# Contractions over 128 rows in four tiles and one bank, projections set ahead, and outputs scaled behind the next block's copies

## The chip, the cores and the metric

One core of one Trainium2 chip runs one program that holds the whole computation. The metric is the device time of one execution in microseconds; the kernel before takes 2904.78 us, the median of three runs. The core has five engines with queues of their own, which run in order: TensorE (matmuls, PE in the profile, with its weight loads as PEld), VectorE (DVE), ScalarE (ACT), GpSimd (POOL) and SyncE (SP). In this kernel SP only issues transfers (DMAs), and POOL issues some and does some arithmetic. Matmuls write into a memory of their own, PSUM, in banks; a bank takes 512 fp32 columns here.

## The reference

Four layers follow each other: attention, a state-space convolution (S4D), attention, and the convolution again, with the same weights in both rounds. Sequence length is 2048, width 640, 32 heads of 20 channels, and 128 states per channel.

```python
def _A_ref(x, wqkv, wo):
    qkv = (x @ wqkv).reshape(B, S, 3, H, Dh)          # q, k, v
    scores = jnp.einsum("bhqd,bhkd->bhqk", q, k) * (Dh ** -0.5)
    p = _softmax(scores, axis=-1)
    o = jnp.einsum("bhqk,bhkd->bhqd", p, v)
    return o.reshape(B, S, D) @ wo

def _B_ref(u, log_A_real, A_imag, C_real, C_imag, log_dt, D_skip):
    P = jnp.exp((A * dt[:, None])[:, :, None] * pos[None, None, :])
    K = 2.0 * jnp.einsum("dn,dnl->dl", C, P).real     # 640 kernels of length 2048
    ...                                               # y = causal convolution of u with K, by FFT
    return y + u * D_skip

x = x + _A_ref(_layernorm(x), A_wqkv, A_wo)
x = x + _B_ref(_layernorm(x), ...)
x = x + _A_ref(_layernorm(x), A_wqkv, A_wo)
x = x + _B_ref(_layernorm(x), ...)
```

## The kernel before

**Attention.** Heads go in groups of four (`g`, 8 groups), queries in blocks of 512 (`qb`, 4 for each group), keys in tiles of 128 (`kt`, 16). A *block* is one group and one query block, 32 of them in a layer. For each key tile there are two *waves* (`j`), each for two heads: `scores` issues eight fp16 matmuls (L769) into one of two score buffers `S` of two banks each, and one exponential on ScalarE (L772) takes it to `pt`. So a layer has 1024 waves, and a key tile is a pair of them. `values` (L786) then multiplies `pt` with the values of the key tile for all four heads, in eight tiles of 64 rows and 32 columns, into two accumulators `pa`; a last column of ones gives the sum that the softmax divides by. When a block ends, DVE copies `pa` into `oc` and adds its two halves (`values`, the part under `kt == NI - 1`). The sums then travel: POOL writes them to memory (`dn<-oc`), loads them in another shape (`dr<-dn`), DVE inverts them, POOL writes them back (`dn<-dr`) and spreads them over partitions (`db<-dn`), DVE scales (`oc<-oc,db`) and POOL stores the output (`ot<-oc`). Each step is a function in the list `later` with the planned time at which it is emitted.

**Work set between the waves.** Two kinds of work share two more banks `m0` and `m1`. *Projections* (`jobs`, L560 and L524): the queries and keys of the later head blocks, 15 steps of eight matmuls into both banks for each 512 columns, 120 steps for a block of 128 channels, and the values of later heads over all 128 rows in one bank. When the queries and keys of a block are done, `norms` (L488) sums their squares, and `shift` writes one number per query and head to memory (`qm<-mr` on POOL). The loads of queries for a head group (`load_q`, on SP) read it again as `qop<-qm`. *Contractions* (`contract`, L322), in the first attention layer alone: the S4D kernel `K` is a sum over 128 states, made of factors that DVE multiplies out (`kgen`, tiles `ka` and `kb`) and TensorE contracts. There are 80 contractions of two halves each. A half has four accumulation steps, for each of which four channels stand in four column tiles and the 128 states are cut into two halves of 64 rows, each with its own bank; DVE copies the first bank to `ko` and adds the second.

**What sets the order.** The program is straight-line. The class `Plan` holds planned times of TensorE, ScalarE and DVE. `slot` puts one step between the waves if it fits before the planned end of the exponential. A contraction is taken first, but only where the planned projection time spent so far (`spent`) has reached `ahead(wave)`, a line through the pairs of wave and microseconds of `AHEAD`; otherwise the next projection step goes. A head group asks (`need`) for its projections ten key tiles into the group's last block before it, and what is missing is then emitted at once. `emptied` notes when each bank is free. TensorE, DVE, POOL and SP keep the order in which the program emits; L74 in the profile is the helper that records every operation of DVE, POOL and SP, so these are told apart by their tiles.

**Behind attention** come the output projection, in the first round together with the transform of the S4D kernel, and then the convolution.

Of the kernel before, what the change touches and what calls it, by code (L numbers as in the profile page):

```python
# [11 lines left out]
F32 = mybir.dt.float32  # L12
# [9 lines left out]
P = 128  # L22
# [7 lines left out]
NA, NB = 32, 64  # L30
LV = [1.0, 2.0, 4.0, 8.0, 16.0, 32.0, 64.0, 128.0, 256.0, 512.0, 1024.0, 1536.0]
PB = 7
AHEAD = ((0, 0.0), (108, 22.0), (364, 47.0), (490, 72.0), (740, 125.0))
WS = 256.0
LG = 2
BOUND = 30.0
# [45 lines left out]
def mha_s4d_kernel(ctx, tc, x_in, wqkv, wo, lar, aim, cr, ci, ldt, dsk,  # L82
                   c_e1, c_eb, c_f2, c_fa, c_sel, c_lv, c_id, c_sg, c_e16, c_f16, c_id16, out, parts="asas", general=None):
    nc = tc.nc
    plan = Plan()
# [8 lines left out]
    se, te = nc.scalar, nc.tensor  # L94
# [11 lines left out]
    def pst(pool, *a, **k):  # L106
        return ps_[pool].tile(*a, **k)
# [68 lines left out]
    def chain(ins):  # L176
        last[0] = tie(ins, last[0])

    def kgen():
# [126 lines left out]
            ve.tensor_mul(ts[3], fa[1], fb[0])  # L306
            yield

        def contract(bs, sub, ko, a, b):

            ps = [pst("M", [P, 512], F32, tag=f"m{r}", name=f"m{r}")[:, :DC // 4 * NB].rearrange("p (c b) -> p c b", b=NB)
                  for r in range(2)]
            for c8 in range(DC // 4):
                if c8:
                    yield plan.pe + 0.7, 0.43, True, ()
                plan.on_pe(0.43)
                for n in range(4):
                    for j in range(4):
                        ch, dd = DC * (sub % 2) + 4 * c8 + j, 4 * c8 + j
                        for r in range(2):  # L320
                            rows = slice(64 * r, 64 * r + 64)
                            chain(te.matmul(ps[r][32 * j:32 * j + 32, c8, :], a[n // 2][rows, ch, :], b[n][rows, dd, :],  # L322
                                            start=(n == 0), stop=(n == 3), tile_position=(64 * r, 32 * j)))
            kos = ko[:, 2 * sub:2 * sub + 2, :]
            emptied(lambda: ve.tensor_copy(kos, ps[0]), lambda: ve.tensor_add(kos, kos, ps[1]))
            if sub == BC // DC - 1:
                ge.dma_start(kd[bs, :].rearrange("(c j) (a b) -> (j a) c b", j=4, b=NB), ko)

# [46 lines left out]
    def emptied(*copies):  # L375

        for r, f in enumerate(copies):
            if f:
                plan.dve = max(plan.dve, plan.pe + 0.25)
                f()  # L380
                free[r] = plan.dve + 0.15
# [12 lines left out]
    def attention(x, stats):  # L394
# [228 lines left out]
        def slot(until=None):  # L623
# [3 lines left out]
            begun = head[0] and head[0][2]  # L627
            if pend and part[0] is None and not begun and (head[0] is None or spent[0] >= ahead(len(ends) - 2)):
                t, f, args = pend[0]
                t = max(t + 0.15, *free)  # L630
                if t <= plan.pe or until is None and head[0] is None:
                    part[:] = f(*args), (t, 0.43, True, ())
                    pend.pop(0)
            step = part[1] if part[0] else head[0]
            if step is None:
# [14 lines left out]
        def drain_later(end=False):  # L650
            send(end)
            while later and (later[0][0] <= plan.pe or end):
                later.pop(0)[1]()
# [103 lines left out]
        plan.keep = True  # L757
        pp = c.enter_context(tc.tile_pool(name="pp", bufs=PB))
        ev = c.enter_context(tc.tile_pool(name="ev", bufs=2))
        ready = []  # L760

        def scores(kt_, kc, qt):

# [14 lines left out]
        def values(qb, g, kt, pts, pa):  # L778
# [10 lines left out]
            if kt == NI - 1:  # L789
# [6 lines left out]
                ve.tensor_copy(oc, pa[0])  # L796
                ve.tensor_add(oc, oc, pa[1])
                sums_[0] = plan.dve + 0.15

                def sums():  # L800
                    for j in range(4):
# [17 lines left out]

                def scale():  # L820
                    ve.tensor_mul(oc, oc, db[0])

                def store():
                    for j in range(4):
                        h = 4 * g + j
                        ge.dma_start(ot[h * DH:(h + 1) * DH, 512 * qb:512 * qb + 512], oc[32 * j:32 * j + DH, :])
                later.extend((plan.dve + n, f) for n, f in (
                    (0.2, sums), (5.0, load), (10.0, invert), (11.0, back), (15.5, spread), (22.5, scale), (23.8, store)))
                later.sort(key=lambda e: e[0])

        def end_jobs():

# [67 lines left out]
                    tail = end_jobs()  # L900
        for r_ in ready:
            values(*r_[1:])
        drain_later(True)
        plan.keep = False
        first.append(split(1))
# [501 lines left out]
```

## Time and profile before

| | |
|---|---|
| median of three runs | 2904.78 us (2903.93 to 2905.59) |
| the profiled execution | 2906.51 us, span 2904.6 us |
| mean granted clock of TensorE | 0.98 |
| waves of the first attention layer, first to last | 119.8 to 1264.4 us |
| waves of the second attention layer | 1687.0 to 2672.7 us |
| ScalarE's exponentials, both layers | 2048 |

The profile is of one execution, which the hardware traces. A row of a group of instructions gives the line, engine and operation, the tiles written and read, the shapes and the count; then the busy time in us and the mean duration in ns; then the idle time of the engine just before these instructions and what ended most of it. A row of a window gives its ends and length in us, the busy time of each engine with its count of instructions, the granted clock, the share of the DMA engines and the GB/s. A row of the timeline gives the start and length in us, the engine, the line, the operation and tiles, how many are merged, and in brackets the idle time before it and what ended it. A row of waits gives the total, the number and the longest. An fp32 matmul of the program stands as two matmul records and two load records in the trace.

### The profile page before, as it was taken

The page shows a single profiled execution, that of the slowest core. Times are in us where ns is not written, and L with a number is a line of the kernel's source. Part 1 is how long each engine was busy: PE and PEld are TensorE (multiplying, and loading weights), DVE is VectorE, ACT ScalarE, POOL GpSimd, SP SyncE. Part 2 cuts the span into 40 slices and gives each one's busy share as a digit, 9 for nine tenths or more (in the row PEclk, how much of TensorE's full clock was granted, in tenths as well). Part 3 has the DMA queues.
Part 4 walks back from the last instruction along what each step waited for, and adds up shares of the span by engine and source line. Part 5 has one row for each costly group of instructions (what it writes and reads, how often), then busy time and mean ns, then how long its engine had stood idle before and what let it go on. Part 6 is the DMA issues. An engine that isn't in the chain of part 4 may idle for free.

```text
span 2904.6 us, 127995 instructions
## 1 busy us (share of the span) xinstructions
PE 2581.2 (89%) x57088; PEld 1537.6 (53%) x57088; DVE 1497.7 (52%) x3333; ACT 2360.6 (81%) x2862; POOL 795.5 (27%) x1229
## 2 busy tenths in 40 slices
PE   7679898998999788789999898999999978878999
PEld 3235555554555444367788554544444433334988
DVE  8555667777775687146777633332222200001865
ACT  5878888998899788855565488999999989998364
POOL 1002223222222222330067012222222332222376
PEclk9889999999999999999999999999999999999999
DMA  5212222222111111335454212121211211112265
GB/s 165 105 55 58 62 59 60 62 53 68 52 55 42 51 41 50 131 119 185 190 188 140 67 35 64 55 65 40 61 46 44 66 28 39 31 43 61 86 204 162
DMA packets 174754, 231.45 MB, mean 80 GB/s; under 512 B 35952, under 2 KB 124336, under 8 KB 172400
## 3 DMA queue, kind: packets, MB, share of 16 engines
q1 hardware_dynamic: 139856, 180.84, 19.2%
q0 software_dynamic: 34336, 42.32, 5.8%
q8 instruction: 450, 7.37, 1.1%
q14 instruction: 112, 0.92, 0.1%
HBM read 150.94 MB, written 72.10 MB: 77 GB/s over the span
## 4 chain that ended last, share of the span: by engine, by line
ACT 26%; PE 18%; issue 6%; DMA 3%; DVE 2%; POOL 1%; SPq 0%; ACTq 0%; POOLq 0%; DVEq 0%
ACT pt L772 25%; PE psv L1135 2%; PE psy L1145 2%; PE po L1041 2%; PE psx L1123 2%; PE psx L1100 2%; PE pst L1110 1%; PE pkf L1015 1%; PE pkx L998 1%; PE pv L524 1%; PE po L1035 1%; PE pa L786 1%; PE pq L682 1%; DMA kl<-kd 1%; PE pkt L1007 1%
## 5 line engine op out<-in xcount | busy, mean ns | idle before, releaser
L772 ACT ACTIVATE pt<-S 128x1024 f32<-128x1024 f32 x2048 | 1932.4, 1040 | 168.2 <-PE S L769 155.1
L786 PE MATMUL pa<-pt,V 64*32 64x512 f32 x16384 | 1144.3, 597 | 17.3 <-DVE oc L74 9.3
L769 PE MATMUL S<-qop,kop 61*32 61x512 f16 x16384 | 921.8, 383 | 184.6 <-ACT pt L772 149.1
L769 PEld LDWEIGHTS <-kop 61*32 61x32 f16 x16384 | 393.8, 90 | 836.9 <-issue 742.5
L786 PEld LDWEIGHTS pa<-pt,V 64*32 64x32 f32 x16384 | 330.1, 107 | 93.7 <-issue 32.0
L74 POOL DMA_DIRECT2D dn<-oc x256 | 126.2, 499 | 446.2 <-DVE oc L74 352.4
L74 POOL DMA_DIRECT2D ot<-oc x256 | 129.2, 512 | 392.5 <-DVE oc L74 313.3
L74 DVE TENSOR_SCALAR qc<-m 128x512 f32<-128x512 f32 x64 | 44.2, 690 | 298.9 <-PE m L560 298.8
L322 PE MATMUL m<-kb,ka 64*32 64x64 f32 x10240 | 158.4, 222 | 44.6 <-issue 42.4
L322 PEld LDWEIGHTS m<-kb,ka 64*32 64x32 f32 x10240 | 150.8, 105 | 82.4 <-issue 65.3
L74 DVE COPY oc<-pa 128x512 f32<-128x512 f32 x64 | 44.2, 691 | 275.0 <-PE pa L786 275.0
L74 POOL DMA_DIRECT2D db<-dn x256 | 128.5, 508 | 133.7 <-DMA dn<-dr 126.0
L74 DVE TENSOR_TENSOR kb<-ktab 128x512 f32<-128x512 f32 x240 | 155.9, 684 | 16.4 <-PE m L322 16.4
L560 PE MATMUL m<-xh,wh 64*32 64x512 f16 x2560 | 148.8, 382 | 12.5 <-DVE qc L74 12.5
L560 PE MATMUL m<-xl,wh 64*32 64x512 f16 x2560 | 148.0, 381 | 0.0
L560 PE MATMUL m<-xh,wl 64*32 64x512 f16 x2560 | 147.0, 380 | 0.2 <-issue 0.2
L560 PEld LDWEIGHTS <-wh 64*32 64x32 f16 x5120 | 97.1, 94 | 79.0 <-issue 42.2
L1128 POOL TENSOR_TENSOR t<-t,kb 128x512 f32<-128x512 f32 x80 | 101.9, 1274 | 71.2 <-DVE t L74 70.3
L1112 ACT COPY xt<-pst 128x1024 f16<-128x1024 f16 x80 | 81.6, 1023 | 46.7 <-PE pst L1110 46.5
L74 DVE TENSOR_SCALAR dr<-dr 128x16 f32<-128x16 f32 x64 | 14.7, 229 | 188.5 <-DMA dr<-dn 188.4
L74 DVE TENSOR_TENSOR oc<-oc,db 128x512 f32<-128x512 f32 x64 | 44.1, 690 | 125.7 <-DMA db<-dn 124.2
L74 POOL DMA_DIRECT2D dn<-dr x64 | 35.6, 556 | 263.8 <-DVE dr L74 256.7
(222 smaller groups left out, 3877.3 us busy)
## 6 DMA issues: line engine op xcount, KB each, us to landing
ka<-kha SPq DMA_DIRECT2D x80, 256.0 KB
kb<-khb SPq DMA_DIRECT2D x80, 256.0 KB
db<-dn POOLq DMA_DIRECT2D x256, 64.0 KB, 2.6
qop<-qs SPq DMA_DIRECT2D x256, 40.0 KB
kop<-ks SPq DMA_DIRECT2D x128, 80.0 KB
ot<-oc POOLq DMA_DIRECT2D x256, 40.0 KB, 2.0
otl<-ot SPq DMA_DIRECT2D x32, 320.0 KB
kha<-kn SPq DMA_DIRECT2D x20, 512.0 KB
```

The costliest lines, as they stand in the source:

```text
L74: made = f(out, *a, **k)
L322: chain(te.matmul(ps[r][32 * j:32 * j + 32, c8, :], a[n // 2][rows, ch, :], b[n][rows, dd, :], start=(n == 0), stop=(n == 3), tile_positio ...
L560: chain(te.matmul(ps[r][32 * t:32 * t + 32, :], a_[rows, ct, 32 * t:32 * t + 32], m[rows, ct, sl], start=(k == 0), stop=(k == 14), tile_po ...
L769: chain(te.matmul(S[32 * t:32 * t + 32, 512 * r:512 * r + 512], kt_[rows, kc + 32 * t:kc + 32 * t + 32], qt[rows, :], start=True, stop=Tru ...
L772: se.activation(pt, S, AF.Exp, scale=SCALE)
L786: chain(te.matmul(pa[r][32 * j:32 * j + 32, :], V[rows, kt, VP * h:VP * h + 32], pts[j // 2][rows, 512 * (j % 2):512 * (j % 2) + 512], sta ...
L1041: te.matmul(pos[hf], oh[:, ct, :], m[:, ct, 320 * hf:320 * hf + 320], start=False, stop=(ct == NCT - 1 and m is wol))
L1100: te.matmul(ps[:, r, i, :], e1[:, e, s, r, :], m[:, s, bs], start=(n == 0), stop=(n == 2))
L1112: se.copy(xt, pt.rearrange("p k g c -> p k (g c)"))
L1123: te.matmul(px, f2[:, f, :], xt[:, k, :], start=(n == 0), stop=(n == 2))
L1128: ge.tensor_mul(t2, t2, kb)
L1135: te.matmul(pv[:, g].rearrange("p r i c -> p (r i c)"), t1[:, g * P:g * P + P], fa, start=True, stop=True)
```

## The change

Three things are changed.

First, a contraction no longer cuts the 128 states in two. Each matmul goes over all 128 rows, in four column tiles, into one bank; the bank `r` is the one that is free first. One DVE copy takes the result, and the add is gone. Second, the waves of `AHEAD` are set some 12 to 16 lower, so that a contraction waits until the projections have come further. Third, the scale of a block's output is no longer timed by `later`: it is kept in `scaled` and emitted behind the copies of the next block, and the store is set 0.3 us behind it. The last block's scale is emitted after the rest of its chain.

```diff
-AHEAD = ((0, 0.0), (108, 22.0), (364, 47.0), (490, 72.0), (740, 125.0))
+AHEAD = ((0, 0.0), (96, 22.0), (352, 47.0), (478, 72.0), (724, 125.0))
...
-        def contract(bs, sub, ko, a, b):
+        def contract(r, bs, sub, ko, a, b):
 
-            ps = [pst("M", [P, 512], F32, tag=f"m{r}", name=f"m{r}")[:, :DC // 4 * NB].rearrange("p (c b) -> p c b", b=NB)
-                  for r in range(2)]
+            ps = pst("M", [P, 512], F32, tag=f"m{r}", name=f"m{r}")[:, :DC // 4 * NB].rearrange("p (c b) -> p c b", b=NB)
...
-                        for r in range(2):
-                            rows = slice(64 * r, 64 * r + 64)
-                            chain(te.matmul(ps[r][32 * j:32 * j + 32, c8, :], a[n // 2][rows, ch, :], b[n][rows, dd, :],
-                                            start=(n == 0), stop=(n == 3), tile_position=(64 * r, 32 * j)))
-            kos = ko[:, 2 * sub:2 * sub + 2, :]
-            emptied(lambda: ve.tensor_copy(kos, ps[0]), lambda: ve.tensor_add(kos, kos, ps[1]))
+                        chain(te.matmul(ps[32 * j:32 * j + 32, c8, :], a[n // 2][:, ch, :], b[n][:, dd, :],
+                                        start=(n == 0), stop=(n == 3), tile_position=(0, 32 * j)))
+            evac = lambda: ve.tensor_copy(ko[:, 2 * sub:2 * sub + 2, :], ps)
+            emptied(*((None, evac) if r else (evac,)))
...
-                t = max(t + 0.15, *free)
+                r = free.index(min(free))
+                t = max(t + 0.15, free[r])
                 if t <= plan.pe or until is None and head[0] is None:
-                    part[:] = f(*args), (t, 0.43, True, ())
+                    part[:] = f(r, *args), (t, 0.43, True, ())
...
                 ve.tensor_add(oc, oc, pa[1])
                 sums_[0] = plan.dve + 0.15
+                if scaled:
+                    scaled.pop()()
...
                 def scale():
                     ve.tensor_mul(oc, oc, db[0])
+                    later.append((plan.dve + 0.3, store))
+                    later.sort(key=lambda e: e[0])
...
-                    (0.2, sums), (5.0, load), (10.0, invert), (11.0, back), (15.5, spread), (22.5, scale), (23.8, store)))
+                    (0.2, sums), (5.0, load), (10.0, invert), (11.0, back), (15.5, spread)))
                 later.sort(key=lambda e: e[0])
+                scaled.append(scale)
...
+        drain_later(True)
+        scaled.pop()()
         drain_later(True)
```

**TensorE, one half of a contraction in the first attention layer.** The first rows are of before: the end of a wave's scores, and the start of the half behind it, which goes on like this for 32 matmuls.

```order
L769 LDWEIGHTS kop_101
L769 MATMUL S<-qop_105,kop_101 32x512
L322 MATMUL m_10977<-kb_10821,ka_10632 32x64
L322 MATMUL m_10978<-kb_10821,ka_10632 32x64
L322 MATMUL m_10977<-kb_10821,ka_10632 32x64
```

And of the change, a whole half and the next wave's first score:

```order
L767 LDWEIGHTS kop_102
L767 MATMUL S<-qop_106,kop_102 32x512
L319 MATMUL m_9779<-kb_9440,ka_9118 32x64 x4
L319 MATMUL m_9779<-kb_9441,ka_9118 32x64 x4
L319 MATMUL m_9779<-kb_9442,ka_9119 32x64 x4
L319 MATMUL m_9779<-kb_9443,ka_9119 32x64 x4
L767 LDWEIGHTS kop_104
L767 MATMUL S<-qop_108,kop_104 32x512
```

The two banks in turn have become one, and 32 matmuls have become 16.

**DVE, the end of the third last block of the first layer** (`oc<-oc,db` is the scale, `oc<-pa` the first copy, `dr<-dr` the inversion). Of before:

```order
L74 TENSOR_SCALAR dr<-dr 128x16
L74 RECIPROCAL dr<-dr 128x16
L74 TENSOR_TENSOR oc<-oc,db 128x512
L74 COPY oc<-pa_28145 128x512
L74 TENSOR_TENSOR oc<-oc,pa_28146 128x512
```

And of the change:

```order
L74 RECIPROCAL dr<-dr 128x16
L74 COPY oc<-pa_25497 128x512
L74 TENSOR_TENSOR oc<-oc,pa_25498 128x512
L74 TENSOR_TENSOR oc<-oc,db 128x512
L74 TENSOR_SCALAR dr<-dr 128x16
```

The scale stood ahead of the next block's two copies and now stands behind them.

**POOL, around the writing of `qm` for the last block of projections** (`k2m` is the maximum over partitions that `shift` needs, `qm<-mr` the writing, `db`, `dn` and `dr` are the chain of a block's sums, `kd` and `kpw` belong to `kgen`). Of before:

```order
L74 DMA dn<-dr 128x16
L74 ISA k2m<-k_23440 128x2
L74 DMA db<-dn 32x512 x4
L74 DMA qm<-mr 7x512 x4
L74 DMA kd<-ko 128x8x64
```

And of the change:

```order
L74 DMA kpw<-wd 128x2x384
L74 ISA k2m<-k_21394 128x2
L74 DMA dr<-dn 128x16
L74 DMA qm<-mr 7x512 x4
L74 DMA dn<-dr 128x16
```

The writing stood behind the spreading of a block's sums; now it stands earlier in the chain, behind the load of an earlier block's sums. In the program the norms of this block of projections are emitted at wave 745 instead of 757; those of the first such block stay at wave 118.

More of the change, by code (lines that the diff above doesn't have):

```diff
@@ L759, in attention @@
         ev = c.enter_context(tc.tile_pool(name="ev", bufs=2))
-        ready = []
+        ready, scaled = [], []
         def scores(kt_, kc, qt):
```

## The prediction

> **What bounds the kernel now.** I read the page first, then three stretches by window, then the waits of ScalarE in them, then the rows around single waits. The profiled execution took 2906.51 us (span 2904.6 us, 1.9 us around it); the median of the runs is 2904.78 us, so what I work out against the execution carries over with 1.7 us taken off.
>
> ```profile
> PE 2581.2 (89%) x57088; PEld 1537.6 (53%) x57088; DVE 1497.7 (52%) x3333; ACT 2360.6 (81%) x2862; POOL 795.5 (27%) x1229
> q8 instruction: 450, 7.37, 1.1%
> L772 ACT ACTIVATE pt<-S 128x1024 f32<-128x1024 f32 x2048 | 1932.4, 1040 | 168.2 <-PE S L769 155.1
> L322 PE MATMUL m<-kb,ka 64*32 64x64 f32 x10240 | 158.4, 222 | 44.6 <-issue 42.4
> L322 PEld LDWEIGHTS m<-kb,ka 64*32 64x32 f32 x10240 | 150.8, 105 | 82.4 <-issue 65.3
> ```
>
> The exponentials (L772) are most of ScalarE's work, one per wave, 1024 waves in each attention layer; 155.1 us of idle time before them waits for the scores on TensorE. The contractions (L322) run in layer 1 alone. TensorE has 114,176 instructions, and queue q8 loads 7.37 MB of program: 64.5 bytes for each, in 450 packets, so a packet holds about 256 of them (worked out; it takes q8 to be TensorE's).
>
> The next windows are two stretches of layer 1 with contractions, one of layer 2 with projections and no contractions, and the start of layer 2's attention; columns PE, PEld, DVE, ACT, POOL. The waits behind them are ScalarE's, in the first three in that order.
>
> ```profile
> 300.00:960.00 660.00, 608.15 (x19711) 354.49 (x19696) 479.00 (x1060) 594.74 (x621) 165.14 (x307) 1.00 0.20 56
> 1000.00:1165.00 165.00, 138.43 (x4956) 79.88 (x4957) 129.32 (x295) 145.09 (x153) 39.57 (x73) 1.00 0.16 44
> 1830.00:2300.00 470.00, 456.02 (x11048) 220.45 (x11048) 141.59 (x270) 465.31 (x495) 116.91 (x231) 1.00 0.18 51
> 1690.00:1770.00 80.00, 77.78 (x2108) 41.18 (x2100) 22.74 (x39) 79.79 (x87) 12.19 (x24) 1.00 0.14 42
> ...
> ACT pt L772 <- PE S L769: 59.9, 59, 2.4
> ...
> ACT pt L772 <- PE S L769: 18.9, 20, 1.7
> ...
> ACT pt L772 <- PE S L769: 10.7, 8, 5.5
> ```
>
> A wave takes 80/87 = 0.92 us where ScalarE is the bound, 470/495 = 0.949 in the mixed stretch of layer 2, but 660/621 = 1.063 and 165/153 = 1.078 us beside contractions. Against 0.92 the two stretches lose 660 - 571.3 = 88.7 and 165 - 140.8 = 24.2 us, **113 us** in 774 waves. The granted clock is 1.00 in all of them. What ends last there is this:
>
> ```profile
> 465.56 0.54 PE L322 MATMUL m<-kb,ka 64*32 64x64 f32 x34 [2.34 <-issue]
> 466.46 2.08 ACT L772 ACTIVATE pt<-S 128x1024 f32<-128x1024 f32 x2 [2.38 <-PE S L769]
> ```
>
> TensorE stands 2.34 us in the middle of a contraction, waiting for no semaphore that the profile shows ("issue"), and ScalarE waits 2.38 us behind it. Over the whole run it stood 42.4 us like this ahead of contraction matmuls (the page's row above), and the 59 waits of ScalarE in the first stretch are of this size, 1.0 us on average. I read it as TensorE running out of loaded instructions: in a pair of waves with a contraction's half it needs 32 score, 32 value and 128 contraction records (loads and matmuls), 192 in 1.84 us, or 104 per us, and the mean of the first stretch, stops included, is 39,407/660 = 60. Layer 2's start took 52.6 per us with no loss.
>
> **The change part by part.**
>
> *Contractions over 128 rows.* A half loses 32 of its 64 matmuls and 32 of its 64 loads. The pair then needs 128 records in 1.84 us, 70 per us, and one packet's worth lasts 3.7 us instead of 2.5. Whether that is enough is not shown directly: the rates seen are 52.6 (no loss) and 60 (with stops). I take nearly all of the stops to go, 8 us of them left; the ends are 0 and 45 us (half of 88.7).
> Against that stands a price. All other work in these waves uses 64-row tiles, so each half goes to 128 rows and back. The trace shows that step for the value projections (L524, 128 rows):
>
> ```profile
> 864.56 1.05 PE L786 MATMUL pa<-pt,V 64*32 64x512 f32 x16
> 865.42 0.41 PE L769 MATMUL S<-qop,kop 61*32 61x512 f16 x8
> 865.76 0.24 PE L524 MATMUL m<-vh,xh 128*128 128x160 f16 x1
> ...
> 866.26 0.23 PE L524 MATMUL m<-vl,xh 128*128 128x160 f16 x1
> 866.42 0.41 PE L769 MATMUL S<-qop,kop 61*32 61x512 f16 x8
> 866.64 1.04 PE L786 MATMUL pa<-pt,V 64*32 64x512 f32 x16
> ```
>
> Scores are followed by values after 866.64 - 866.42 = 0.22 us, but by the 128-row projection after 0.34: 0.12 us in. Out it is 0.16 instead of 0.07: 0.09 us. So 0.21 us a visit, and 160 halves make 34 us of TensorE time. The half itself now takes some 0.57 us:
>
> ```profile
> 510.07 0.79 PE L322 MATMUL m<-kb,ka 64*32 64x64 f32 x61
> 510.64 0.38 PE L769 MATMUL S<-qop,kop 61*32 61x512 f16 x1
> ```
>
> I leave it at 0.57: half the matmuls, but four run together instead of eight. A pair then costs TensorE 0.22 + 0.22 + 0.86 (865.42 - 864.56) + 0.57 + 0.21 = 2.08 us against 1.84 of ScalarE. Scores have two buffers, and pairs without contractions give some back; of the 34 us I count 16, with 0 and 34 as ends.
> The Trainium skill says in "TensorEngine Tiling (Array Packing)", section Key Properties, that changing the tiling mode, and not just the tile, drains TensorE. The trace agrees, at 0.21 us a visit; the page has no figure. By the rule read strictly, nothing hides, and the sum would be 18 us higher.
> One DVE add per contraction goes too, 80 in all, 0.29 us each (961.21 below); DVE is not the bound, so I count nothing, between 0 and 23 us.
>
> What stays above 0.92 without stops is the mixture of layer 2, 0.949 - 0.92 = 0.03 us in 774 waves, 23 us. Sum: 113 - 23 - 16 - 8 = **66 us** gained; with the ends together 113 - 23 = 90 down to 113 - 23 - 34 - 45 = 11.
>
> *Projections set ahead.* The last projection block's norms stand at wave 745 in the program instead of 757; the loads of queries for the seventh head group stand at wave 756. Now they collide:
>
> ```profile
> 961.21 0.29 DVE L74 TENSOR_TENSOR ko<-ko,m 128x128 f32<-128x128 f32 x1
> ...
> 962.23 1.09 SPq L74 DMA_DIRECT2D qop<-qs  x2
> 979.35 0.21 SPq L74 DMA_DIRECT2D qop<-qm  x1
> ...
> 975.53 2.07 POOL L74 DMA_DIRECT2D qm<-mr  x4
> ...
> 989.53 1.22 PE L769 MATMUL S<-qop,kop 61*32 61x512 f16 x8 [8.16 <-DMA qop<-qm]
> ...
> 990.87 1.02 ACT L772 ACTIVATE pt<-S 128x1024 f32<-128x1024 f32 x1 [8.38 <-PE S L769]
> 993.00 2.85 ACT L772 ACTIVATE pt<-S 128x1024 f32<-128x1024 f32 x3 [1.11 <-PE S L769]
> 996.97 1.02 ACT L772 ACTIVATE pt<-S 128x1024 f32<-128x1024 f32 x1 [1.11 <-PE S L769]
> ```
>
> SP stood 16 us at the load of qm, whose writing was queued on POOL behind the db transfers of a block; TensorE then lacked 8.16 us. Twelve waves are 11 us, more than that, and on POOL the writing no longer stands behind db: 8.4 + 1.1 + 1.1 = 10.6, **11 us** (0 if SP is late for another reason). At the first such boundary the norms stay at wave 118; 13 of the 15 forced projection steps before them are now done earlier, 13 x 0.22 = **3 us**. What the earlier projections push back is little: 6 contraction halves instead of 8 stand in the first 128 waves, and the last one stands at wave 905 instead of 929.
>
> *Outputs scaled later.* DVE now does a block's copies before the scale of the block ahead. The scale waited for its db:
>
> ```profile
> 1201.44 0.69 DVE L74 TENSOR_TENSOR oc<-oc,db 128x512 f32<-128x512 f32 x1 [9.55 <-DMA db<-dn]
> 1202.79 2.72 PE L786 MATMUL pa<-pt,V 64*32 64x512 f32 x16 [4.52 <-DVE oc L74]
> 1206.07 1.02 ACT L772 ACTIVATE pt<-S 128x1024 f32<-128x1024 f32 x1 [6.43 <-PE S L769]
> ...
> 2340.13 0.69 DVE L74 TENSOR_TENSOR oc<-oc,db 128x512 f32<-128x512 f32 x1 [7.80 <-DMA db<-dn]
> 2345.11 1.02 ACT L772 ACTIVATE pt<-S 128x1024 f32<-128x1024 f32 x1 [7.06 <-PE S L769]
> ```
>
> In these two places the copies behind it, then the values, then ScalarE waited: 6.43 + 7.06 = 13.5, **14 us** with the slower waves behind. Elsewhere DVE waits alone. Two smaller moves have a row each:
>
> ```profile
> 1274.98 0.55 POOL L74 DMA_DIRECT2D dr<-dn  x1 [5.75 <-DMA dn<-oc]
> ...
> 2615.02 1.55 ACT L943 CAST oh<-otl 128x640 fp32r<-128x640 f32 x2 [3.79 <-issue]
> ```
>
> The four output stores now stand on POOL between the next block's sums and the load of those sums, which waits 5.75 us for them anyway: nothing, and 2 us off the path without that cover. ScalarE's first two casts for the output projection stand five waves later in layer 2, where they waited 3.79 us, and two to four waves earlier in layer 1; **2 us** gained, between -3 and 4.
>
> Sum: 66 + 11 + 3 + 14 + 2 = 96 us. 2904.8 - 96 = **2809 us**.
>
> **The rivals.** *The stops stay in part*: a packet in 3.7 us is still too often. Half of 88.7 stays, 45 instead of 8: 2846 us. For it speaks that no stretch shows 70 per us without loss.
> *DVE becomes the bound*: it is busy 129.32/153 = 0.845 us a wave in the second stretch, 92% of 0.92, and it stands in order behind each contraction's result.
>
> ```profile
> DVE ko L74 <- PE m L322: 88.4, 71, 3.6
> ```
>
> That wait is 1.2 us on average, and the stretch holds 20 contractions (2,524 matmul records by 128): 20 x 1.2/153 = 0.16, together 1.0 us a wave. In all 774 waves that is 774 us against my 712 + 47 = 759 (47 = 23 + 16 + 8), so 2824 us. Against it: most of that wait is TensorE's stop, which goes.
> *Slower: weights no longer load under a matmul.* With one row group, each of the 8 rounds of a half (four accumulation steps, and an fp32 matmul is two records) would pay a load and a matmul, 0.105 + 0.222, or 2.6 us; a pair would take 1.30 + 2.6 + 0.21 = 4.1 us, 160 x 2.27 = 363 us lost instead of 90: 2904.8 + 363 - 90 - 30 = 3148 us. It decides from a half of 1.3 us on (120 us over 160 pairs, 0.75 above 1.84). Against it are these rows of full 128-row tiles:
>
> ```profile
> L1145 PEld LDWEIGHTS psy<-v,eb 128*128 128x128 f32 x224 | 26.1, 192 | 0.0
> ...
> 2830.83 1.95 PE L1145 MATMUL psy<-v,eb 128*128 128x128 f32 x16
> ```
>
> Sixteen take 1.95 us, 0.12 each, while one load lasts 0.192: loads do run under matmuls there. The Trainium skill, "TensorE: Matmul & The Clock Gate", section Part 3, lets a load overlap a running matmul only where the row group differs; by that rule this rival would come, and the trace speaks against the rule.
> *It does not do what it says*: stops depend on something else than the count and stay whole, and all drains count: 2904.8 - 30 + 34 = 2909 us, no change.
>
> **How the numbers follow.** Forecast 0.58; stops in part 0.18; DVE 0.14; slower by loads 0.05; no effect 0.05. The range runs from all drains hidden and no stop left (24 us below, 2785) with 7 us for the adds and casts, 2778, to the stops in part with all drains counted, 2864. Faster 0.91 (the first three and a little of the last), same 0.03, slower 0.06. Under 0.2%, 6 us, counts as no change, about what a measurement of this kernel can tell.
>
> **What would show it.** In the changed profile "issue" before the contraction falls from 42.4 us to under 8; ScalarE waits under 30 us in the stretches of contractions; waves take some 0.98 us; a contraction half is followed by scores after some 0.6 to 0.8 us; no wait for qop at the seventh group; no wait for oc on TensorE. I am wrong if a half takes over 1.3 us, if TensorE waits for kb, or if "issue" stays.

## The result, and the profile after

The changed kernel takes **2797.37 us**, the median of four runs (2796.54 to 2802.16), beside 2904.36 us for the kernel before on the same chip. The ratio is 0.9632, with a 95% interval of 0.962 to 0.9644: some 107 us, 3.7%, are gone. The prediction was 2809 us, with a range of 2778 to 2864. The profiled execution took 2797.11 us, its span 2795.1 us, 109.5 us less than before's.

These rows of the page answer to the first ones of before (L770 is the exponential, L767 the scores, L319 the contraction, L784 the values):

```profile
PE 2550.9 (91%) x51968; PEld 1441.8 (52%) x51968; DVE 1465.2 (52%) x3253; ACT 2356.1 (84%) x2862; POOL 794.9 (28%) x1229
q8 instruction: 410, 6.72, 1.0%
L770 ACT ACTIVATE pt<-S 128x1024 f32<-128x1024 f32 x2048 | 1927.9, 1040 | 62.9 <-PE S L767 48.4
L319 PEld LDWEIGHTS m<-kb,ka 128*32 128x32 f32 x5120 | 79.1, 110 | 86.9 <-issue 64.6
L319 PE MATMUL m<-kb,ka 128*32 128x64 f32 x5120 | 104.9, 222 | 1.0 <-DVE qc L74 1.0
```

"issue" ahead of contraction matmuls was 42.4 us and is gone: the 1.0 us left waits for DVE. ScalarE waited 155.1 us for scores and now waits 48.4; these 107 us are nearly the whole gain. Queue q8 loads 40 packets fewer. The "issue" ahead of the weight loads (65.3 us, now 64.6) did not move, and so says nothing of the stops.

The windows of the two stretches with contractions, and under them ScalarE's wait for scores from 290 to 890 us:

```profile
290.00:896.00 606.00, 598.73 (x16704) 293.33 (x16689) 491.34 (x1076) 592.97 (x621) 171.16 (x316) 1.00 0.23 63
935.00:1069.00 134.00, 121.04 (x3256) 53.80 (x3241) 91.60 (x207) 132.83 (x142) 36.32 (x63) 1.00 0.24 66
...
ACT pt L770 <- PE S L767: 10.8, 9, 5.8
```

A wave takes 606/621 = 0.976 and 134/142 = 0.944 us, against 1.063 and 1.078 before. The chain of starts of the exponentials in the two traces says where the 109.5 us lie. Each line is a stretch of waves of the first layer (0 to 1023) and the second (from 1024), and what it takes less than before:

| waves | us gained | what stands there |
|---|---|---|
| 0 to 130 | 8.0 | first boundary of projections |
| 130 to 756 | 58.1 | contractions |
| 756 to 776 | 11.7 | the wait for `qop` at the seventh head group |
| 776 to 930 | 20.9 | contractions |
| 930 to 1023 | -0.5 | end of layer 1: one stall gone, two new |
| 1690 to 1705 | 7.7 | the stall behind a scale in layer 2 |
| all else | 3.6 | |

The two new stalls at the end of layer 1 look like this (timeline of the changed kernel, POOL, DVE, TensorE and ScalarE):

```profile
1067.40 3.04 POOL L931 TENSOR_TENSOR wol<-wot,woh 128x640 fp32r<-128x640 f32 x2
1069.16 1.98 DVE L74 TENSOR_SCALAR dr<-dr 128x16 f32<-128x16 f32 x1 [23.70 <-DMA dr<-dn]
1071.38 0.69 DVE L74 COPY oc<-pa 128x512 f32<-128x512 f32 x1
1072.13 1.43 PE L784 MATMUL pa<-pt,V 64*32 64x512 f32 x12 [1.95 <-DVE oc L74]
1074.33 34.32 ACT L770 ACTIVATE pt<-S 128x1024 f32<-128x1024 f32 x37 [2.78 <-PE S L767]
...
1111.71 0.72 ACT L948 CAST oh<-otl 128x640 fp32r<-128x640 f32 x1 [3.07 <-issue]
1113.85 0.72 ACT L948 CAST oh<-otl 128x640 fp32r<-128x640 f32 x1 [1.42 <-DMA otl<-ot]
```

First, POOL casts the output weights (`wol`, `woh`), the sums of a block wait behind that, DVE's inversion `dr` waits 23.70 us for the sums, the next block's copies stand behind it on DVE, and ScalarE loses 2.78 us. Little of this is POOL's work: behind its first cast of 0.72 us it stands idle for 10.13 us, and the profile names nothing that it waits for; then come the first subtraction, 1.55 us, and the load of the sums. Second, ScalarE's own casts of `oh` stand ahead of exponentials. The second one waits for its load `otl<-ot`; for the first the profile names nothing, but it starts 3.67 us behind the issue of its load. From 1112 to 1122 us, behind this stall, the granted clock is 0.50, and ScalarE waits 1.11 us more; the expectations below call that the clock's tail.

### The profile page after: what moved, and what is told of

Same layout as the page of the kernel before. It is cut to its first block, busy times and chain, and to the rows that moved or that the text cites. A ratio compares the mean times of both kernels' runs of the same rounds, so it can differ in the third digit from the quotient of the medians.

```text
span 2795.1 us, 117550 instructions
## 1 busy us (share of the span) xinstructions
PE 2550.9 (91%) x51968; PEld 1441.8 (52%) x51968; DVE 1465.2 (52%) x3253; ACT 2356.1 (84%) x2862; POOL 794.9 (28%) x1229
## 4 chain that ended last, share of the span: by engine, by line
ACT 53%; PE 25%; issue 12%; DVE 4%; DMA 4%; POOL 1%; SPq 0%; ACTq 0%; DVEq 0%; POOLq 0%
ACT pt L770 53%; PE pa L784 3%; PE po L1046 3%; PE psv L1140 2%; PE psy L1150 2%; PE S L767 2%; PE psx L1128 2%; PE psx L1105 2%; PE po L1040 1%; PE pv L521 1%; PE pst L1115 1%; PE m L557 1%; PE pkf L1020 1%; PE pkx L1003 1%; DMA kop<-ks 1%
## 5 line engine op out<-in xcount | busy, mean ns | idle before, releaser
L770 ACT ACTIVATE pt<-S 128x1024 f32<-128x1024 f32 x2048 | 1927.9, 1040 | 62.9 <-PE S L767 48.4
L784 PE MATMUL pa<-pt,V 64*32 64x512 f32 x16384 | 1101.3, 594 | 2.1 <-DVE oc L74 1.9
L767 PE MATMUL S<-qop,kop 61*32 61x512 f16 x16384 | 869.7, 383 | 168.4 <-ACT pt L770 148.6
L767 PEld LDWEIGHTS <-kop 61*32 61x32 f16 x16384 | 371.0, 90 | 840.8 <-issue 735.8
L784 PEld LDWEIGHTS pa<-pt,V 64*32 64x32 f32 x16384 | 310.2, 107 | 73.4 <-issue 11.6
L557 PE MATMUL m<-xh,wh 64*32 64x512 f16 x2560 | 138.5, 381 | 12.1 <-DVE qc L74 12.1
L557 PE MATMUL m<-xl,wh 64*32 64x512 f16 x2560 | 137.4, 379 | 0.0
L557 PEld LDWEIGHTS <-wh 64*32 64x32 f16 x5120 | 87.7, 94 | 82.2 <-issue 44.5
L319 PEld LDWEIGHTS m<-kb,ka 128*32 128x32 f32 x5120 | 79.1, 110 | 86.9 <-issue 64.6
L1117 ACT COPY xt<-pst 128x1024 f16<-128x1024 f16 x80 | 81.6, 1023 | 46.7 <-PE pst L1115 46.5
L319 PE MATMUL m<-kb,ka 128*32 128x64 f32 x5120 | 104.9, 222 | 1.0 <-DVE qc L74 1.0
L1134 POOL TENSOR_TENSOR t<-t,t 128x512 f32<-128x512 f32 x78 | 99.1, 1270 | 7.3 <-DVE t L74 1.3
```

What stands on the lines that cost most here:

```text
L319: chain(te.matmul(ps[32 * j:32 * j + 32, c8, :], a[n // 2][:, ch, :], b[n][:, dd, :], start=(n == 0), stop=(n == 3), tile_position=(0, 32 ...
L557: chain(te.matmul(ps[r][32 * t:32 * t + 32, :], a_[rows, ct, 32 * t:32 * t + 32], m[rows, ct, sl], start=(k == 0), stop=(k == 14), tile_po ...
L767: chain(te.matmul(S[32 * t:32 * t + 32, 512 * r:512 * r + 512], kt_[rows, kc + 32 * t:kc + 32 * t + 32], qt[rows, :], start=True, stop=Tru ...
L770: se.activation(pt, S, AF.Exp, scale=SCALE)
L784: chain(te.matmul(pa[r][32 * j:32 * j + 32, :], V[rows, kt, VP * h:VP * h + 32], pts[j // 2][rows, 512 * (j % 2):512 * (j % 2) + 512], sta ...
L1117: se.copy(xt, pt.rearrange("p k g c -> p k (g c)"))
```

## The experiments

Each kernel was timed beside the kernel before on its own chip; a ratio is to that. "Trace" is the span of the profiled execution against 2795.1 us of the changed kernel, or 2904.6 of before.

| run | median us | ratio, 95% interval | trace |
|---|---|---|---|
| changed kernel | 2797.37 | 0.9632 (0.962 to 0.9644) | |
| e1, first part alone | 2830.33 | 0.9744 (0.9728 to 0.9761) | 79.5 us under before |
| e9, second part alone | 2898.76 | 0.9968 (0.9953 to 0.9983) | 7.2 us under before |
| e10, third part alone | 2891.27 | 0.9941 (0.992 to 0.9962) | 10.8 us under before |
| e2, second part undone | 2803.39 | 0.9648 (0.9634 to 0.9662) | 10.0 us over changed |
| e3, third part undone | 2823.89 | 0.9728 (0.9705 to 0.9751) | 25.0 us over changed |
| e4, half columns | 2869.95 | 0.9875 (0.9856 to 0.9893) | 76.3 us over changed |
| e8, one visit | 2817.37 | 0.97 (0.9686 to 0.9713) | 20.7 us over changed |
| e12, price told | 2796.30 | 0.9617 (0.9598 to 0.9637) | 2.6 us over changed |
| e5, casts in place | 2810.64 | 0.968 (0.9666 to 0.9694) | 10.8 us over changed |
| e6, POOL casts tied | 2789.34 | 0.9607 (0.9594 to 0.9621) | 9.9 us under changed |
| e7, both | 2805.35 | 0.9656 (0.9642 to 0.9669) | 10.6 us over changed |
| e11, casts mended | 2780.16 | 0.956 (0.9541 to 0.9579) | 13.5 us under changed |

### The parts alone, and undone

**e1, the first part alone** (the changed kernel with `AHEAD` and the scale as before):

```diff
+AHEAD = ((0, 0.0), (108, 22.0), (364, 47.0), (490, 72.0), (740, 125.0))
...
-                if scaled:
-                    scaled.pop()()
...
+                    (0.2, sums), (5.0, load), (10.0, invert), (11.0, back), (15.5, spread), (22.5, scale), (23.8, store)))
```

> The kernel before with the first part of the change alone: contractions over 128 rows in one bank; AHEAD and the scale's place are those of before. Theory (fewer instructions, so TensorE no longer runs out of them): nearly the whole gain of the two stretches comes, some 79 us as the trace of the changed kernel shows it, so 2820 to 2832 us; idle time 'issue' ahead of contraction matmuls falls from 42.4 us to under 8. The wait for qop at the seventh head group (8 us) and the two waits behind scales stay. Rival (the stretches gain because the projections are further ahead): under 45 us gained, 2860 us or more. Rival (the parts carry each other, the gain is less than the sum): between these.

1 - 0.9744 of 2904.8 us are 74 us, 70% of the whole gain. "issue" ahead of contraction matmuls was gone (of the 1.5 us left there, 1.3 wait for DVE). But the wait for `qop` at the seventh head group, which was to stay, went too: by the trace, waves 756 to 776 took 11.5 us less than before with the old `AHEAD`.

**e9, the second part alone** (the kernel before, new `AHEAD`):

> The kernel before with the second part of the change alone, the new waves of AHEAD. By the prediction the wait for qop at the seventh head group goes (8.2 us and some clock tail) and a little at the first boundary: 11 + 3 = 14 us, ratio 0.995 (2893 us). The run without the new AHEAD showed that with the short contractions this wait goes by itself; if the new AHEAD is worth anything for it, it must be here. Rival: the contractions, longer in this kernel, are pushed back (the last from wave 929 to 992, into the last block), and the stops and the work behind them eat the gain: ratio 1.000 within 0.003.

0.9968 is 9 us, between the two. Waves 756 to 776 took 11.6 us less, as predicted for this part, and waves 130 to 756 took 13.4 us less, since fewer contractions stand there. But the last contraction moved from wave 929 to 992, and from wave 970 to 1023 the kernel lost 32 us again. These are ScalarE's waits from 1160 to 1265 us, of e9 and then of before:

```profile
ACT pt L772 <- PE S L769: 21.4, 10, 14.3
ACT oh L943 <- DMA otl<-ot: 14.7, 1, 14.7
...
ACT pt L772 <- PE S L769: 8.7, 4, 6.4
ACT oh L943 <- DMA otl<-ot: 1.3, 1, 1.3
```

**e2, the second part undone** (the changed kernel, old `AHEAD`):

> The changed kernel with the waves of AHEAD as they were before. Theory: the loads of queries for the seventh head group meet the late writing of qm again, 8 us of wait for qop and some clock tail, 11 us, and 3 to 5 us at the first boundary: 2808 to 2814 us. Rival (with shorter contractions the projections are in time by themselves, and the numbers of AHEAD are worth nothing): 2797 us within 6, and no wait for qop over 2 us.

The ratio is 0.0016 above that of the changed kernel, 5 us, and the intervals overlap; the one profiled execution is 10.0 us longer. The wait at the seventh head group did not come back. Here is the writing of `qm` on POOL and TensorE's wait for it, in before, in e2 and in the changed kernel (shortest, median and longest duration in ns, first and last start in us; then who waited, how long in us and how often):

```profile
L74 POOL DMA_DIRECT2D qm<-mr x4: 518/525/532, 975.5 to 977.1; - x4
  PE S L769: 8.2, 1
...
L74 POOL DMA_DIRECT2D qm<-mr x4: 518/530/538, 906.9 to 908.5; - x4
  PE S L767: 1.8, 1
...
L74 POOL DMA_DIRECT2D qm<-mr x4: 518/523/556, 900.5 to 902.1; - x4
  PE S L767: 0.5, 1
```

In the program the norms of the last projection block stand at wave 757 before, 737 in e9, 739 in e1, 751 in e2 and 745 in the changed kernel. So either part is enough: by the program's rule a contraction that needs one free bank leaves room for projections earlier, and so do the new numbers of `AHEAD`. What was to be 11 us of the second part is shared.

**e10, the third part alone** (the kernel before, the scale behind the next copies):

> The kernel before with the third part of the change alone: the scale of a block behind the copies of the next, and the store behind it. By the prediction both stalls behind a scale go, 14 us, ratio 0.995. In the changed kernel the undoing of this part cost some 25 us, since there the sums of the third last block were held up on GpSimd by the casts of the output weights; here the stalls are 6.4 and 7.1 us, so if only they count, 12 to 15 us; if the later store makes the first casts of the output projection late as in the changed kernel, 6 to 9 us, ratio 0.997.

0.9941 is 17 us, 11 to 23 by the interval, so the 14 us of the two stalls lie within it. By the trace 7.7 us of it came at the scale in layer 2 (waves 1690 to 1705). In layer 1 the stall of 6.43 us went too, but the casts of `oh` now wait 2.92 and 1.49 us there, as in the changed kernel, where in before they waited 1.3.

**e3, the third part undone** (the changed kernel, the scale timed as before):

> The changed kernel with each scale timed in the list 22.5 us behind its block, as before. By the prediction both stalls behind a scale come back, 14 us: 2811 us. By the trace of the changed kernel only layer 2's 7.8 us came home, since in layer 1 a new wait of 2.9 us for oc and a later start of the casts took the rest: 2803 to 2806 us, the new wait for oc near wave 930 gone. Rival (the place of the scale is worth nothing, db now comes in time anyway): 2797 us within 6.

0.9728, 28 us: twice what the prediction said, and no rival had it. Most of it is one stall at the end of layer 1, waves 930 to 960:

```profile
1069.03 2.08 DVE L74 TENSOR_SCALAR dr<-dr 128x16 f32<-128x16 f32 x1 [23.43 <-DMA dr<-dn]
1077.70 2.02 POOL L74 DMA_DIRECT2D db<-dn  x4 [1.60 <-DMA dn<-dr]
1084.86 0.69 DVE L74 TENSOR_TENSOR oc<-oc,db 128x512 f32<-128x512 f32 x1 [13.46 <-DMA db<-dn]
1086.20 2.73 PE L784 MATMUL pa<-pt,V 64*32 64x512 f32 x16 [15.87 <-DVE oc L74]
1089.48 1.02 ACT L770 ACTIVATE pt<-S 128x1024 f32<-128x1024 f32 x1 [17.77 <-PE S L767]
```

The inversion is as late as in the changed kernel (1069.03 against 1069.16 us), since the same casts on POOL hold up the sums. There the copies stand right behind it and ScalarE loses 2.78 us. Here the scale stands between, waits for the whole way through memory, and ScalarE loses 17.77.

### Where the stops come from

**e4, half columns.** The same contraction with the instruction count of before:

```diff
-                for n in range(4):
-                    for j in range(4):
...
-                        chain(te.matmul(ps[32 * j:32 * j + 32, c8, :], a[n // 2][:, ch, :], b[n][:, dd, :],
+                for s in (slice(0, NB // 2), slice(NB // 2, NB)):
+                    for n in range(4):
+                        for j in range(4):
...
+                            chain(te.matmul(ps[32 * j:32 * j + 32, c8, s], a[n // 2][:, ch, :], b[n][:, dd, s],
```

> The changed kernel, but every contraction matmul (128 rows, 64 columns moved) is issued as two of 32 columns each: the same sums, the same bank, the same one DVE copy and the same two mode changes for a half, with the instruction count of before (128 records a half instead of 64). Theory (TensorE runs out of loaded instructions): the stops are back, 'issue' ahead of contraction matmuls 30 to 50 us, ScalarE waiting over 60 us in the stretches, 2860 to 2890 us. Rival (the gain came from the freed bank, the missing add or the planner's shorter wait): no stops, 2797 us within 8. Third case (matmuls of 32 columns make a half longer): no 'issue', a half followed by scores only after 0.8 us or more instead of 0.58, and 2810 to 2850 us.

It lost 71 us by the ratio. The page's row of the contraction, q8, TensorE's and ScalarE's waits from 290 to 890 us, and then one half with a stop and one without:

```profile
L320 PE MATMUL m<-kb,ka 128*32 128x32 f32 x10240 | 131.8, 200 | 28.0 <-issue 26.7
q8 instruction: 450, 7.37, 1.1%
...
PE m L320 <- issue: 20.8, 22, 1.6
ACT pt L771 <- PE S L768: 59.2, 62, 4.1
...
371.72 0.40 PE L768 MATMUL S<-qop,kop 61*32 61x512 f16 x8
372.05 0.58 PE L320 MATMUL m<-kb,ka 128*32 128x32 f32 x42
374.20 0.39 PE L320 MATMUL m<-kb,ka 128*32 128x32 f32 x22 [1.57 <-issue]
374.52 0.41 PE L768 MATMUL S<-qop,kop 61*32 61x512 f16 x8
...
375.94 0.76 PE L320 MATMUL m<-kb,ka 128*32 128x32 f32 x64
376.63 0.41 PE L768 MATMUL S<-qop,kop 61*32 61x512 f16 x8
```

The bank, the one copy and the mode changes are those of the changed kernel, yet the stops are back inside the halves, and ScalarE waits 59.2 us in the window where the changed kernel has 10.8. Before had 63.4 there. A half without a stop has become longer, 376.63 - 375.94 = 0.69 us against 0.58, which is 160 x 0.11 = 18 us of TensorE time at most. So some 53 to 71 of the 71 us go with the number of instructions. That it is the loading of the instructions can be read from where and when TensorE stops. Count its records (matmuls, loads and those of its sequencer) in order of their starts. All 46 stops over 0.5 us that name no semaphore in before (53.0 us together, with some ahead of scores and values) stand ahead of record 193 or 194 of each 256, the number that a packet of q8 holds by the prediction's working; so do all 27 in e4. Each ends 1.2 to 1.6 us behind the end of one of q8's packets. In the changed kernel, from 290 to 890 us, TensorE reaches this place a median of 2.74 us behind the packet, where before has 1.72, and it does not stop there.

**e8, one visit.** Both halves of a contraction are issued together:

```diff
-            for c8 in range(DC // 4):
-                if c8:
-                    yield plan.pe + 0.7, 0.43, True, ()
-                plan.on_pe(0.43)
+            plan.on_pe(0.86)
+            for c8 in range(DC // 4):
```

> The changed kernel, but the two halves of a contraction are issued in one visit: 80 visits of 32 program matmuls instead of 160 of 16, the same matmuls, half the mode changes. If what the drains cost is TensorE time that adds up over the stretch (0.21 us a visit, 80 visits fewer): 17 us less TensorE time, up to 13 us faster, since ScalarE waits for 13 us there in all: 2784 to 2795 us. Rival (a visit of some 1.2 us overruns the two score buffers each time: a pair takes 0.22 + 0.33 + 1.17 + 0.86 = 2.58 us, and two pairs 2.58 + 1.84 = 4.42 against 4.00 now): up to 80 times 0.42 = 34 us slower, 2805 to 2831 us.

The rival was right, 20 us slower. TensorE's timeline of the changed kernel, and then of e8:

```profile
441.41 0.40 PE L767 MATMUL S<-qop,kop 61*32 61x512 f16 x8
441.74 0.65 PE L319 MATMUL m<-kb,ka 128*32 128x64 f32 x32
442.32 0.41 PE L767 MATMUL S<-qop,kop 61*32 61x512 f16 x8
442.55 1.04 PE L784 MATMUL pa<-pt,V 64*32 64x512 f32 x16
443.41 0.40 PE L767 MATMUL S<-qop,kop 61*32 61x512 f16 x8
...
446.01 0.40 PE L767 MATMUL S<-qop,kop 61*32 61x512 f16 x8
446.33 1.10 PE L319 MATMUL m<-kb,ka 128*32 128x64 f32 x64
447.37 0.41 PE L767 MATMUL S<-qop,kop 61*32 61x512 f16 x8
447.59 1.04 PE L784 MATMUL pa<-pt,V 64*32 64x512 f32 x16
448.45 0.40 PE L767 MATMUL S<-qop,kop 61*32 61x512 f16 x8
```

One half, with the step out of 128 rows, takes 0.58 us (442.32 - 441.74); two take 1.04 (447.37 - 446.33). So a half is 0.45 to 0.46 and the step out 0.12 to 0.13; the step in is 0.33 - 0.22 = 0.11. A visit's two mode changes cost some **0.24 us** by this working, and 80 fewer visits would spare TensorE some 19 us (an estimate, 80 x 0.24). But a pair then takes 448.45 - 446.01 = 2.44 us instead of 2.00, and the two score buffers do not carry ScalarE over that: from 290 to 890 us it waits 27.4 us for scores, 62 times, where the changed kernel has 10.8, 9 times.

**e12, price told.** The planned time of a half, 0.43 us, is set to 0.6:

> The changed kernel with the planned time of a contraction's half set to 0.6 us instead of 0.43 (measured with its mode changes: 0.69). The program then sets halves only where more room is planned; the last one stands at wave 937 instead of 905. Theory (a pair with a half takes 2.00 us since the planner sets it into 1.84, and places with more room exist): up to 10 us faster, 2787 to 2794 us. Rival (there is no place with more room, every pair looks alike, and each half costs its 0.16 us wherever it stands): 2797 us within 4. Third case (the halves pushed back into waves 905 to 937 meet the end of the layer's other work): 2801 to 2810 us.

No difference that can be measured: 0.9617 (0.9598 to 0.9637) and 0.9632 (0.962 to 0.9644) overlap. The last half stands at wave 937 instead of 905, and waves 130 to 905 take as long (753.4 us in the changed kernel, 753.7 here).

### The stalls that are left

**e6, POOL's casts tied** into the order of the program:

```diff
-                ge.tensor_copy(woh[:, ct, :], wt)
-                ge.tensor_sub(wol[:, ct, :], wt, woh[:, ct, :])
+                ge.last = tie(ge.tensor_copy(woh[:, ct, :], wt), ge.last)
+                ge.last = tie(ge.tensor_sub(wol[:, ct, :], wt, woh[:, ct, :]), ge.last)
```

> The changed kernel, but GpSimd's five casts and five subtractions of the output weights (woh, wol) are tied into the order in which the program emits its other work: all ten behind a block's db transfers and ahead of the next block's sums, instead of between dn, dr and db. Theory (these stand ahead of the load dr<-dn, DVE's inversion waits 24 us for it, and the copies of the next block stand behind the inversion): the 2.8 us wait for oc at 1074 us goes, 2793 to 2795 us. Rival (GpSimd's ten operations take as long wherever they stand and delay the next block's sums as much): 2797 us within 3.

0.9607 against 0.9632, 7 us, with intervals that just overlap. By the trace the wait at 1074 us went (3 us of the span); the rest of its 9.9 us lies in small steps all over, and is not explained.

**e5, ScalarE's casts in place, and e7, both.** ScalarE's first casts are tied behind the exponential that is emitted ahead of them:

```diff
+            lastexp[0] = se.activation(pt, S, AF.Exp, scale=SCALE).ins
...
+        first.append(split(1))
         plan.keep = False
-        first.append(split(1))
...
-            se.copy(oh, cur)
+            tie(se.copy(oh, cur), lastexp[0] if plan.keep else None)
```

> The changed kernel, but ScalarE's first casts for the output projection (oh<-otl) are tied behind the exponential that the program emits ahead of them, so the first stands at wave 1014 and the second behind the last wave, instead of both at wave 970 or so of 1024. Theory (in both layers ScalarE's queue stands still because these casts are ahead of exponentials and their loads come late): the stalls of 5.2 to 6.0 us and the clock's tail of 1.1 to 1.2 us behind each go, 13 us less 1.5 us for two casts that now stand behind the waves: 2784 to 2788 us. Rival (the load's lateness comes back as a wait at the start of the output projection): 2797 us within 4.

> The changed kernel with both: ScalarE's casts tied behind the waves and GpSimd's casts tied into the program's order. If the two stalls are independent, 13 + 3 us less 1.5: 2781 to 2785 us. If one hides the other, 2784 to 2788 us.

Both were slower than without this edit, by 14 us each (e5 against the changed kernel, e7 against e6). The last wave of layer 1 started 9.5 us sooner in e5 and the waves of layer 2 gained 6 us, as the theory has it, but behind the two layers' waves 10.6 and 14.8 us were lost. The timeline of e5 behind layer 1:

```profile
1176.08 0.69 DVE L74 TENSOR_TENSOR oc<-oc,db 128x512 f32<-128x512 f32 x1 [5.92 <-DMA db<-dn]
1176.69 0.82 DVE L74 TENSOR_TENSOR ol<-otl,oh 128x640 fp32r<-128x640 f32 x1
1177.56 2.63 PEld L1041 LDWEIGHTS po<-woh,ol 128*128 128x128 f32 x10 [15.35 <-DVE ol L74]
```

With `plan.keep` left on, DVE's subtraction `ol` for the second cast was tied too, and stood behind the last block's scale; the output projection waited 15.35 us for it. The fault was in the edit, not in the casts' place.

**e11, casts mended**: e6's edit, and only the casts of ScalarE tied, with `plan.keep` as it was:

> The changed kernel with GpSimd's casts tied into the program's order, as in the run before that was faster, and with ScalarE's two casts tied behind exponentials (the first at wave 1014, the second behind the last wave), but without the side effect of the earlier try, which had also put DVE's subtraction for the second cast behind the last block's scale. Theory (in the earlier try the waves ended 9.5 us sooner in layer 1 and some 5 us sooner in layer 2, and all of it and more was lost because TensorE waited 15 us for that subtraction): now the gain stays, 12 to 14 us on top of the 7 to 8 of GpSimd's casts: 2775 to 2780 us, ratio 0.956 to 0.958. Rival (the output projection has to wait for the last block's output in any case, so that earlier waves are worth nothing): 2789 us within 4, ratio 0.961.

0.956 (0.9541 to 0.9579), 21 us under the changed kernel by the ratios: **the fastest of all, 2780 us**. Here are ScalarE's waits from 1062 to 1166 us, of the changed kernel and then of e11 (the row of e11 is behind the last wave):

```profile
ACT pt L770 <- PE S L767: 4.5, 3, 2.8
ACT oh L948 <- issue: 3.1, 1, 3.1
ACT oh L948 <- DMA otl<-ot: 1.4, 1, 1.4
...
ACT oh L949 <- PE po L1047: 5.2, 1, 5.2
```

Nothing is waited for among these waves any more.

## Why the prediction was right, step by step

**What bounds it.** Right. The gain lies where the prediction put it: ScalarE's waits for TensorE in the two stretches.

**Contractions over 128 rows, forecast 66 us.** 79 us came in the two stretches (58.1 + 20.9), 68 in e1 alone (51.0 + 16.7 in the same waves), so the mechanism held and the size was a little low. Of its terms, the 8 us of stops that were to stay are none. In before two packets of q8 start no closer than 3.23 us in the first layer's waves; a packet that lasts 2.5 us, as the prediction worked out, is then used up too soon, and one that lasts 3.7 is not. (The stop of 2.34 us that the prediction shows is the longest of its stretch, and not of the size of the mean wait, 1.0.) The 16 us for mode changes are about the size of what is left: against the 0.949 us of the mixture, the first stretch has 606 - 621 x 0.949 = 17 us too much and the second nothing. That these 17 us are the mode changes is not shown; fewer visits (e8) and other places for them (e12) brought nothing. A visit was put at 0.57 + 0.21 us and is 0.45 + 0.24, so a pair takes 2.00 us and not 2.08. The Trainium skill, "TensorEngine Tiling (Array Packing)", section Key Properties, says that a change of tiling mode drains TensorE; the runs agree in so far as the change costs time, 0.24 us for going and coming back. e4 shows the reason itself: the count of instructions restored, and nothing else of the three parts, brings 71 us back, at most 18 of them by longer halves, and the stops stand where a packet of instructions ends.

**Projections ahead, forecast 11 + 3 us.** The wait for `qop` at the seventh group went (11.7 us in the table above), but the step that put this down to the twelve waves of `AHEAD` failed: e1 and e2 show it gone with the old numbers. The 3 us at the first boundary were too few: 8.0 came there, and 5 of them are what the part is worth on top of the first (e2, by its trace; its ratio is not clear of that of the changed kernel). Alone it gives 9 (e9), since there the contractions reach into the last block and ScalarE's casts wait 14.7 us for their load.

**Scale later, forecast 14 us.** 17 us alone (e10), 28 when undone (e3). The prediction counted the two stalls that it saw, and not why the chain was late there. In before too POOL's casts stand just ahead of both: POOL is idle for 8.46 us before its first subtraction at 1184.23 us in layer 1, and for 9.84 before the one at 2314.08 in layer 2. So the scale's place is worth what these casts happen to add to the chain: the stall behind the scale in layer 1 is 6.43 us in before and 17.77 in e3, where the changed kernel has 2.78.

**Casts two to four waves earlier in layer 1 and five later in layer 2, forecast 2 us.** This step failed, in its sign: some 3 us were lost, the lower end that the prediction gave. Layer 2's wait stayed (3.60 us, five waves later in the program, beside 3.79). In layer 1 the casts came to wait 3.07 and 1.42 us, where in before the first waited 1.3 and the second not at all. The step counted waves and not what the casts wait for. In before the loads of `otl` issue at waves 970 and 971 and the casts start at 972 and 974; in the changed kernel both loads and both casts stand at wave 970. SP issues these loads late: in three waits it stands 4.6 us for the stores of a block on POOL (1060 to 1112 us).

```profile
1104.51 2.03 POOL L74 DMA_DIRECT2D ot<-oc  x4
1108.04 0.95 SPq L74 DMA_DIRECT2D otl<-ot  x2
```

The later store is not the whole cause: in e3, with the store in its old place, the loads issue 17 us behind the stores, and the first cast, right behind its load, still waits 3.52 us.

e11 against e6 shows what the place of ScalarE's casts is worth: 0.956 against 0.9607, some 14 us by the ratios (9 by the medians, 3.6 by the two profiled executions).

**The rivals and the signs.** No stops stayed in part. DVE is no bound: it is busy 491.34 of 606 us, and TensorE waits 1.0 us for it ahead of contractions. Of the signs that were named, one did not come: TensorE still waits for `oc`, 1.95 us at 1072 us. Loads do run under matmuls: 32 records of a half start within 0.45 us, with 32 loads of 0.110 us (the row of the profile) beside them, 3.5 us if they stood between. (The half of 1.3 us from which the prediction lets this rival decide has the mode changes in it; without them 1.84 + 0.75 - 1.30 - 0.21 = 1.08.) By the Trainium skill, "TensorE: Matmul & The Clock Gate", section Part 3, a load overlaps a running matmul only where the row group differs; here all have the same, and the measurement decides against the rule for these tiles.

The three parts alone sum to 74 + 9 + 17 = 100 us, beside 107 for all. That is nearly the sum, but by two errors against each other: one wait is removed by two parts, and the third part is worth more beside the first two than alone. The forecast of 96 us is near 107 by luck in part as well: the contractions and the first boundary gave more than they were given, and the casts at the end of layer 1 took some of it back.

## What to carry to other kernels

Where TensorE stops in the middle of a group and the profile names no semaphore, count instructions, and look whether the stops stand at a fixed place of every 256: half as many matmuls, each over twice the rows, gained 74 us here though each visit paid 0.24 us for the change of mode. An operation that waits for a way through memory belongs behind everything on its engine that others wait for; how long it may hold them up is not told by the stalls of one trace alone: ask what else can come into that way. And where an operation that waits for a load is moved, look at when that load can issue.

## What was not expected of the hardware

A matmul with 32 columns moved is not half of one with 64: 64 of them take 0.69 us in e4 where 32 with 64 columns take 0.58, both with the step out, the same columns in all. Fewer mode changes did not help where they made longer bursts: e8 has half of them, 19 us of TensorE's time by the estimate, and was 20 us slower, with pairs of 2.44 us where two score buffers had carried ScalarE over most of the pairs of 2.00. And POOL stands idle ahead of its first subtraction of the output weights in both layers, from 7.1 us (e6, layer 1) to 11.2 us (e1, layer 1), with nothing named that it waits for; why is open.
